# The low part of each gate product on GpSimd, half passes in groups of six, and three smaller moves

## The chip, the cores and the metric

One core of a Trainium2 chip. The metric is the device time of one execution in microseconds, the median of several runs. The engines are named as in the profile: PE is TensorE (matrix products; PEld its weight loads), DVE is VectorE, ACT is ScalarE, POOL is GpSimd, SP is SyncE, which here only issues DMAs.

## What is computed

Cut to what matters, `x` is 2048 tokens of 448 features:

```python
xn = layernorm(x)
a  = irfft2(rfft2(xn) * (w_r + 1j * w_i), s=(2048, 448))   # 2048 x 225 spectral weights
h  = relu(xn @ W_gate) * (xn @ W_up)                        # 448 x 1792 each
return x + a + h @ W_down                                   # 1792 x 448
```

All of it is done in float32 accuracy from float16 products: each operand is split into a high and a low float16 part, and three products (high·high, high·low, low·high) are summed in PSUM.

## The kernel before, in words

Two jobs share the engines. The foreground is the gated feed-forward part. The 1792 hidden features are 14 blocks of 128, in groups of 5, 5 and 4; the tokens are four chunks `q` of 512, in the order 0, 2, 1, 3. A *unit* `(f, q)` is one block for one chunk: ten products for the gate and ten for the up half (`gu_full`, L712), each 128 rows by 512 columns. For every group and chunk the units of the group are followed, a little later, by four *down* products (`dn_mm`, L775), 448 columns wide, which read the high and low part of all the group's units.

448 features are three and a half tiles of 128 rows, in a high and a low part. The odd half tiles are products with 64 rows, the *half passes* (`gu_half`, L718): one gate and one up half pass for each unit, on different rows of TensorE, so that two can run at once. They stand in groups: the first unit of a pair does its full products, then come the half passes of its mate (which opens the mate's PSUM banks) and its own, then the mate's full products (`gu_halves`, L740). `mates` (L969) holds the pairs.

After a unit, `gu_post` (L766) makes its result: ScalarE takes the rectified gate out of PSUM (`gu_relu`, L752), VectorE multiplies by the up half (`gu_times`, L756), ScalarE writes the float16 high part `h` (`gu_hi`, L760), and VectorE the low part, the difference (`gu_lo`, L764). The first five units belong to an opening that is written out by hand (`OPENING`).

PSUM has eight banks: two buffers of two banks for units (`gu`), two for down products (`dn`), two for the background (`fx`).

The background is the layer norm of the later chunks and the Fourier part. It is a list of small steps (`bg`); `run_bg` puts so many of them behind each unit that VectorE's time, by a table of costs, is a fixed share of TensorE's (`fixed`, `room`, L1096 to L1110). Its butterflies (`bfly`, L391) work on 18 buffers with a list of free ones. `swap` (L539) and `row_in` (L556) copy rows between partitions by DMAs.

GpSimd has little to do: small copies in the layer norm (`ln_copy`, `ln_copy_lo`), some fills, and one sum over all partitions (`all_sum`, L188) for each block of gate and up weights, for each group of down weights and for the spectral weights. These all-reduces give the scales: ScalarE squares the weights (L186), GpSimd sums, VectorE turns the sum into a power of two (L192, L196) with which the weights are then split.

Each engine works through its own instructions in the order in which a scheduler put them when the program was built; between engines there are semaphores.

Of the kernel before, what the change touches and what calls it, by code (L numbers as in the profile page):

```python
# [133 lines left out]
def tile_gfnet_reglu(ctx: ExitStack, tc: tile.TileContext, x, xr, wgu, wd, wf, wrow, ident, c_fd, c_fm, c_im, c_row, c_id,  # L134
# [10 lines left out]
    def fx():  # L145
        return psum.tile([128, 512], F32, name="fx", bufs=2)
# [184 lines left out]
    def ln_tp(n2, tiles):  # L331
        if n2 not in tp:
            tp[n2] = fx().bitcast(F16).rearrange("p (a b) -> p a b", b=128)
        for a in tiles:
            P.transpose(tp[n2][:, a, :], tt[n2][:, a, :], id_t)
# [9 lines left out]

    zps, eo, X, Xh, yps, cur = {}, {}, {}, {}, {}, {}

    def f_dft(n2):
        q, j = n2 % 4, n2 // 4
        js = slice(128 * j, 128 * (j + 1))  # L350
        ps = fx()
# [33 lines left out]
    def f_sdft(n2):  # L385
        y = yps[n2] = fx()[:, 0:XW].rearrange("p (g c k) -> p g c k", g=4, c=2)
        m, xh = fm_t[n2 % 8][:, n2 // 8], Xh[n2 % 8][:, n2 // 8]
        for i, (a, b) in enumerate(((0, 0), (0, 1), (1, 0))):
            P.matmul(y, m[:, a, :], xh[:, b], start=(i == 0), stop=(i == 2), skip_group_check=True)  # L389

    def bfly(a, b, p, sgn):  # L391

        if p == 0:
            t = free.pop()
            V.tensor_tensor(t, a, b, op=OP.add)  # L395
            V.tensor_tensor(b, a, b, op=OP.subtract)  # L396
            free.append(a)
            return t, b
        t = free.pop()
        if p == 4:  # L400
# [5 lines left out]
            free.append(b)  # L406
# [132 lines left out]
    def swap(key, k):  # L539
# [27 lines left out]
    def row_dft(d):  # L567
        y = state["rowps"] = fx()
# [35 lines left out]
    def i_sdft(n2):  # L604
        ps = fx()
# [20 lines left out]
    def i_ddft(n2):  # L626
        ps = fx()
# [81 lines left out]
    def gu_open(f, q):  # L709
        hps[f, q] = psum.tile([128, 2, 512], F32, name="gu", bufs=2)  # L710

    def gu_full(f, q, gs, cs, start, stop, seq=SEQ):  # L712
        for g in gs:
            for i, (a, b) in enumerate(seq):
                last["P"] = P.matmul(hps[f, q][:, g, cs], wt[f, g][:, a, :], Tq[q][:, b, cs],  # L715
                                     start=(start and i == 0), stop=(stop and i == len(seq) - 1)).ins

    def gu_half(f, q, g, start, prev):  # L718
# [3 lines left out]
        m = P.matmul(hps[f, q][:, g, 0:512], wt[f, g][rows, 7, :], Tq[q][rows, b, :], start=start, stop=not start).ins  # L722
# [7 lines left out]
    def gu_unit(f, q, mate):  # L730
# [7 lines left out]
        gu_halves(f, q, mate)  # L738
# [11 lines left out]
    def gu_relu(f, q):  # L750
        g1s[f, q] = mt([128, 512], F32, "g1", 3)
        last["A"] = A.activation(g1s[f, q], hps[f, q][:, 0, :], AF.Relu, scale=2.0 ** -22).ins  # L752

    def gu_times(f, q):
        g1 = g1s[f, q]
        last["V"] = V.scalar_tensor_tensor(g1, hps[f, q][:, 1, :], 2.0 ** -22, g1, op0=OP.mult, op1=OP.mult).ins  # L756
# [5 lines left out]
    def gu_lo(f, q):  # L762
        h = ht[f, q]
        V.tensor_tensor(h[:, 1, :], g1s.pop((f, q)), h[:, 0, :], op=OP.subtract)  # L764
# [10 lines left out]
    def dn_mm(fs, n2, c0=0, c1=D):  # L775
        q, j = n2 % 4, n2 // 4
        js = slice(128 * j, 128 * (j + 1))
        ps = psum.tile([128, 512], F32, name="dn", bufs=2)
# [180 lines left out]
    gseq = [("gu", g, f, q) for g, fs in enumerate(groups) for q in CHUNKS for f in fs]  # L959
    units, pend = [], []  # L960
    for k, u in enumerate(gseq):
        units.append(u)
        if k % 2 and pend:
# [5 lines left out]
    mates = {u: v for u, v in zip(gseq[::2], gseq[1::2])}  # L969
# [80 lines left out]
    def gu_slab(f, g):  # L1050
        if f % 2 == 0 and g == 0:
            gu_open(f, q)
        gu_full(f, q, (g,), slice(0, 512), f % 2 == 0, f % 2 == 1)

    for f in groups[0]:
# [9 lines left out]
        if f % 2 == 0:  # L1065
            piece(f"hp{f}", gu_halves, f, q, mates["gu", 0, f, q][2:])
# [13 lines left out]
    with tc.manual_schedule(engines={mybir.EngineType.PE, mybir.EngineType.DVE, mybir.EngineType.Activation,  # L1080
# [3 lines left out]
        wps = psum.tile([128, 512], F32, name="dn", bufs=2)  # L1084
# [11 lines left out]
    def fixed(i):  # L1096
        c = 1.37 if units[i][0] == "gu" else 0.68
# [21 lines left out]
    for i, u in list(enumerate(units))[len(groups[0]):]:  # L1119
        is_gu = u[0] == "gu"  # L1120
        parts = [(0, D)] if i < len(units) - 1 else [(0, CUT), (CUT, D)]
        if is_gu:
            _, g, f, q = u
            run_bg(until=marks["T", q])
            gu_unit(f, q, (mates.get(u) or (0, 0, None, None))[2:])
# [74 lines left out]
```

## Time and profile before

| | us |
|---|---|
| median of 3 runs (446.71 to 446.97) | 446.72 |
| the profiled execution's own time | 446.92 |
| its span | 445.1 |
| TensorE busy | 438.4 (98%) |
| VectorE busy | 373.5 (84%) |
| ScalarE busy | 178.9 (40%) |
| GpSimd busy | 32.9 (7%) |

The span runs from the first to the last instruction of the profiled execution; 1.8 us of its time lie around it. In the lines of groups the columns are: source line, engine, operation, what it writes from what, shape and count; then busy microseconds and mean nanoseconds of one; then the idle time ahead of them and who ended it. In the lines of the timeline and of the chain they are start and length in microseconds. Where several instructions that follow each other make one line, the length goes from the first one's start to the last one's end. TensorE's products overlap each other, so their rate is read from starts and not from lengths.

### The profile page before, as it was taken

How to read it: one execution, taken by the hardware profiler on the slowest of the kernel's cores; microseconds unless marked ns; L12 is line 12 of the kernel's file. 1: busy time of each engine (PE TensorE's matmuls, PEld its weight loads, DVE VectorE, ACT ScalarE, POOL GpSimd, SP SyncE). 2: the span in 40 equal slices, each digit the busy share in tenths (PEclk: the TensorE clock that was granted, in tenths of full speed). 3: DMA queues.
4: the chain of work that ended last, by engine and by line, in shares of the span. 5: the costliest groups of instructions: out<-in, count | busy, mean ns of one | idle time of the engine just before them, and what ended most of it. 6: DMA issues, size and time to landing. Idle time of an engine off the chain costs nothing.

```text
span 445.1 us, 7091 instructions
## 1 busy us (share of the span) xinstructions
PE 438.4 (98%) x2630; PEld 218.8 (49%) x2630; DVE 373.5 (84%) x802; ACT 178.9 (40%) x365; POOL 32.9 (7%) x97
## 2 busy tenths in 40 slices
PE   8999999999999999999999999999999999999997
PEld 3543554444546444444444444444444455556565
DVE  5988696998858979999999999896997997766364
ACT  5886252351543666043233145344142242233230
POOL 2431031040000120000000010000000000000000
DMA  8929966041001261432220021000001333231113
GB/s 271 323 52 282 371 217 119 1 90 41 0 14 61 95 222 34 133 105 62 85 80 6 1 84 55 0 13 0 14 0 42 93 96 90 55 96 34 63 43 124
DMA packets 37115, 39.72 MB, mean 89 GB/s; under 512 B 17927, under 2 KB 32473, under 8 KB 37081
## 3 DMA queue, kind: packets, MB, share of 16 engines
q1 hardware_dynamic: 35928, 37.40, 27.4%
q10 hardware_dynamic: 1152, 1.87, 2.1%
q8 instruction: 20, 0.33, 0.3%
q14 instruction: 15, 0.11, 0.1%
HBM read 24.45 MB, written 3.67 MB: 63 GB/s over the span
## 4 chain that ended last, share of the span: by engine, by line
PE 91%; DVE 3%; DMA 2%; ACT 1%; issue 1%; POOL 1%; SPq 0%; ACTq 0%
PE gu L715 50%; PE dn L783 29%; PE gu L722 3%; PE fx L611 2%; PE fx L357 2%; PE fx L632 2%; PE fx L389 2%; DMA y<-in_xr 1%; DMA T<-tt 1%; DVE bst L248 1%; DVE wt L669 1%; DVE y L291 0%; DVE g L756 0%; ACT T L341 0%; DVE tt L320 0%
## 5 line engine op out<-in xcount | busy, mean ns | idle before, releaser
L715 PE MATMUL gu<-T,wt 128*128 128x512 f16 (+1 forms) x1140 | 256.1, 375 | 0.0
L715 PEld LDWEIGHTS <-wt 128*128 128x128 f16 x1140 | 108.7, 98 | 129.8 <-issue 9.3
L783 PE MATMUL dn<-wdt,h 128*128 128x448 f16 (+2 forms) x684 | 136.4, 349 | 0.0
L783 PEld LDWEIGHTS <-h 128*128 128x128 f16 x684 | 65.8, 98 | 59.9
L752 ACT ACTIVATE g<-gu 128x512 f32<-128x512 f32 x56 | 33.2, 594 | 115.1 <-PE gu L722 77.4
L760 ACT ACTIVATE h<-g 128x512 f16<-128x512 f32 x56 | 35.0, 627 | 47.3 <-DVE g L756 47.3
L756 DVE SCALAR_TENSOR_TENSOR g<-gu,g 128x512 f32<-128x512 f32 x56 | 38.5, 687 | 11.4 <-ACT g L752 11.3
L790 DVE SCALAR_TENSOR_TENSOR xy<-dn,dsc,xy 128x448 f32<-128x448 f32 (+2 forms) x49 | 32.9, 671 | 15.1 <-PE dn L783 14.8
L764 DVE TENSOR_TENSOR h<-g,h 128x512 f16<-128x512 f32 x56 | 38.5, 689 | 4.9 <-ACT h L760 4.8
L665 ACT ACTIVATE wt<-wst,wsc 128x512 f16<-128x512 f32 x28 | 19.1, 716 | 15.7 <-DVE wsc L196 15.7
L669 DVE SCALAR_TENSOR_TENSOR wt<-wst,wsc,wt 128x512 f16<-128x512 f32 x28 | 20.5, 749 | 0.0
L637 DVE SCALAR_TENSOR_TENSOR xy<-fx,fsc,xy 128x448 f32<-128x448 f32 x16 | 10.8, 681 | 10.7 <-PE fx L632 10.7
L189 POOL PARTITION_ALL_REDUCE wm<-wm x15 | 7.8, 521 | 158.9 <-ACT junk L186 158.9
L396 DVE TENSOR_TENSOR y<-y 128x456 f32<-128x456 f32 x22 | 13.9, 631 | 4.8 <-DMA row<-y 4.5
L722 PE MATMUL gu<-T,wt 64*128 64x512 f16 x112 | 17.0, 381 | 0.8 <-DMA T<-tt 0.7
L186 ACT ACTIVATE junk<-wst 128x512 bf16<-128x512 f32 x28 | 17.4, 622 | 0.2
L595 ACT ACTIVATE vt<-y,fsc 128x912 f16<-128x912 f32 x8 | 8.4, 1052 | 20.7 <-PE fx L611 12.3
L618 ACT ACTIVATE wf<-fx 114x512 f16<-114x512 f32 x16 | 9.4, 588 | 17.4 <-PE fx L611 16.6
L553 DVE TENSOR_TENSOR y<-y,sw 128x456 f32<-128x456 f32 x16 | 10.1, 628 | 5.7 <-DMA sw<-y 5.7
L395 DVE TENSOR_TENSOR y<-y 128x456 f32<-128x456 f32 x22 | 13.8, 628 | 0.2
L611 PEld LDWEIGHTS <-vt 128*128 128x128 f16 x192 | 12.0, 98 | 3.3
L611 PE MATMUL fx<-wf,vt 128*128 128x128 f16 x192 | 13.2, 219 | 0.0
(115 smaller groups left out, 431.4 us busy)
## 6 DMA issues: line engine op xcount, KB each, us to landing
wst<-in_wgu SPq DMA_DIRECT2D x28, 256.0 KB
wf<-in_wf SPq DMA_DIRECT2D x8, 456.0 KB
sw<-y SPq DMA_DIRECT2D x16, 224.4 KB
y<-in_xr SPq DMA_DIRECT2D x16, 224.0 KB
xy<-in_x SPq DMA_DIRECT2D x16, 224.0 KB
out<-xy SPq DMA_DIRECT2D x15, 224.0 KB
wdst<-in_wd SPq DMA_DIRECT2D x14, 224.0 KB
sw<-y SPq DMA_DIRECT2D x8, 228.0 KB
```

What stands on the lines that cost most here:

```text
L186: A.activation(o, src, AF.Square, scale=SQ, accum_out=acc)
L611: P.matmul(o, v[:, h, w], m[:, c, :], start=(i == 0), stop=(i == 2), skip_group_check=True)
L665: A.activation(w[:, 0:4, :], wst[f, g], AF.Copy, scale=wsc[f, g])
L669: V.scalar_tensor_tensor(w[:, 4:8, :], st, sc, w[:, 0:4, :], op0=OP.mult, op1=OP.subtract)
L715: last["P"] = P.matmul(hps[f, q][:, g, cs], wt[f, g][:, a, :], Tq[q][:, b, cs], start=(start and i == 0), stop=(stop and i == len(seq) - 1 ...
L722: m = P.matmul(hps[f, q][:, g, 0:512], wt[f, g][rows, 7, :], Tq[q][rows, b, :], start=start, stop=not start).ins
L752: last["A"] = A.activation(g1s[f, q], hps[f, q][:, 0, :], AF.Relu, scale=2.0 ** -22).ins
L756: last["V"] = V.scalar_tensor_tensor(g1, hps[f, q][:, 1, :], 2.0 ** -22, g1, op0=OP.mult, op1=OP.mult).ins
L760: A.activation(ht[f, q][:, 0, :], g1s[f, q], AF.Copy)
L764: V.tensor_tensor(h[:, 1, :], g1s.pop((f, q)), h[:, 0, :], op=OP.subtract)
L783: last["P"] = P.matmul(ps[:, 0:c1 - c0], ht[f, q][:, a, js], wdt[f][:, b, c0:c1], start=(i == 0), stop=(i == n - 1)).ins
L790: last["V"] = V.scalar_tensor_tensor(o, dps[n2][:, 0:c1 - c0], dsc[:, g:g + 1], o, op0=OP.mult, op1=OP.add).ins
```

## The change

Five edits:

1. The low part (`gu_lo`) of every unit after the opening is a GpSimd instruction instead of a VectorE one.
2. The half passes stand in groups of three units (six half passes) instead of two, but for the first two and the last two groups. Units and down products share a ring of six single banks, since three units are open at once. Full products are held behind the group's last half pass.
3. In butterflies without a twiddle factor the difference goes over the first operand instead of the second, and freed buffers go to the other end of the list.
4. One of two copies of the forward swap and the copies of `row_in` are issued from ScalarE's queue instead of SP's.
5. The planner charges a unit 0.69 us of VectorE's time instead of 1.37, and asks for 6 us more room.

```diff
-        return psum.tile([128, 512], F32, name="fx", bufs=2)
+    RINGS = {'gu': ('gu', 6), 'dn': ('gu', 6), 'fx': ('fx', 2)}
+    def bank(name="fx"):
+        tag, n = RINGS[name]
+        return psum.tile([128, 512], F32, name=name, tag=tag, bufs=n)
...
     def bfly(a, b, p, sgn):
         if p == 0:
             t = free.pop()
             V.tensor_tensor(t, a, b, op=OP.add)
-            V.tensor_tensor(b, a, b, op=OP.subtract)
-            free.append(a)
-            return t, b
+            V.tensor_tensor(a, a, b, op=OP.subtract)
+            free.insert(0, b)
+            return t, a
...
         if key == "X":
             nc.sync.dma_start(t[1:64], u[65:128])
-            nc.sync.dma_start(t[64:128], u[0:64])
+            nc.scalar.dma_start(t[64:128], u[0:64])
...
-            nc.sync.dma_start(row[p:p + 8, 0, :], cur["s1", j, par][64:65].rearrange("p g c k -> p (g c) k"))
+            nc.scalar.dma_start(row[p:p + 8, 0, :], cur["s1", j, par][64:65].rearrange("p g c k -> p (g c) k"))
...
     def gu_open(f, q):
-        hps[f, q] = psum.tile([128, 2, 512], F32, name="gu", bufs=2)
+        hps[f, q] = [bank("gu") for g in range(2)]
...
-    def gu_halves(f, q, mate):
-        gu_open(*mate)
+    def gu_halves(f, q, mates):
         m = last["P"]
-        for i in range(4):
+        vs = [v[2:] for v in mates] + [(f, q)]
+        for i in range(2 * len(vs)):
+            v = vs[i // 2]
+            if i % 2 == 0 and v != (f, q):
+                gu_open(*v)
+                opened.add(v)
             with tc.high_priority(offset=2000 if i else 0):
-                m = gu_half(*((f, q) if i > 1 else mate), 1 - i % 2, i < 2, m)
-        opened.add(mate)
+                m = gu_half(*v, 1 - i % 2, v != (f, q), m)
+        last["half"] = m
...
     def gu_lo(f, q):
         h = ht[f, q]
-        V.tensor_tensor(h[:, 1, :], g1s.pop((f, q)), h[:, 0, :], op=OP.subtract)
+        e = G if "opened" in state and q in CHUNKS else V
+        e.tensor_tensor(h[:, 1, :], g1s.pop((f, q)), h[:, 0, :], op=OP.subtract)
...
+    for n in [2, 2] + [3] * 16 + [2, 2]:
+        mates[gseq[k]] = gseq[k + 1:k + n]
...
     def fixed(i):
-        c = 1.37 if units[i][0] == "gu" else 0.68
+        c = 0.69 if units[i][0] == "gu" else 0.68
...
-        lo, hi = (m, hi) if sum(room(i, m) for i in range(RAMP, last_gu)) < need else (lo, m)
+        lo, hi = (m, hi) if sum(room(i, m) for i in range(RAMP, last_gu)) < need + 6.0 else (lo, m)
```

The new kernel's line numbers are up to 14 higher: L764 becomes L773, L722 becomes L726, L189 becomes L192.

Two places show what the scheduler made of it. The first is TensorE at a group of half passes for chunk 2, with the numbers of the tiles. Before, two units' half passes stand together, the gate and up half of each in one two-bank tile:

```order
L722 LDWEIGHTS wt_423
L722 MATMUL gu_868<-T2_63,wt_423 128x512
L722 LDWEIGHTS wt_401
L722 MATMUL gu_868<-T2_63,wt_401 128x512
L722 LDWEIGHTS wt_326
L722 MATMUL gu_847<-T2_63,wt_326 128x512
L722 LDWEIGHTS wt_314
L722 MATMUL gu_847<-T2_63,wt_314 128x512
```

Now those of three units, each half with a bank of its own:

```order
L726 MATMUL gu_928<-T2_63,wt_422 128x512
L726 LDWEIGHTS wt_456
L726 MATMUL gu_927<-T2_63,wt_456 128x512
L726 LDWEIGHTS wt_546
L726 MATMUL gu_932<-T2_63,wt_546 128x512
L726 LDWEIGHTS wt_520
L726 MATMUL gu_931<-T2_63,wt_520 128x512
L726 LDWEIGHTS wt_425
L726 MATMUL gu_906<-T2_63,wt_425 128x512
L726 LDWEIGHTS wt_403
L726 MATMUL gu_905<-T2_63,wt_403 128x512
```

So there are 20 groups in place of 28, with the same 112 half passes.

The second is GpSimd where the all-reduces for the last four blocks' weights stand. Rows with `ISA` and a `wm` tile are the all-reduces. Before, they follow each other, between that for the down weights of the second group (`wdm_2099`) and that of the third (`wdm_3289`):

```order
L189 ISA wdm_2099<-wdm_2099 128x5
L189 ISA wm_2852<-wm_2852 128x2
L189 ISA wm_2902<-wm_2902 128x2
L189 ISA wm_2945<-wm_2945 128x2
L189 ISA wm_3088<-wm_3088 128x2
L189 ISA wdm_3289<-wdm_3289 128x4
```

Now the low parts (L773, into an `h` tile) stand among them. The rows `ISA` without a tile name one of two libraries of GpSimd code, which the program puts ahead of an instruction whose code is in the other one: the all-reduce's is library 1, the subtraction's library 0.

```order
L773 TENSOR_TENSOR h_2837<-g1_2834,h_2837 128x512
L192 ISA
L192 ISA wm_2950<-wm_2950 128x2
L773 ISA
L773 TENSOR_TENSOR h_2875<-g1_2872,h_2875 128x512
L192 ISA
L192 ISA wm_2993<-wm_2993 128x2
L773 ISA
L773 TENSOR_TENSOR h_2915<-g1_2912,h_2915 128x512
L773 TENSOR_TENSOR h_2967<-g1_2964,h_2967 128x512
```

Between any all-reduce and a low part there is now such a row: 26 in all, against one before, which stands ahead of the first all-reduce in the opening.

More of the change, by code (lines that the diff above doesn't have):

```diff
@@ L626, in i_ddft @@
     def i_ddft(n2):
-        ps = fx()
+        ps = bank()
         h = pgh[n2]
@@ L714, in gu_full @@
             for i, (a, b) in enumerate(seq):
-                last["P"] = P.matmul(hps[f, q][:, g, cs], wt[f, g][:, a, :], Tq[q][:, b, cs],
+                m = last["P"] = P.matmul(hps[f, q][g][:, cs], wt[f, g][:, a, :], Tq[q][:, b, cs],
                                      start=(start and i == 0), stop=(stop and i == len(seq) - 1)).ins
+                if "opened" in state and "half" in last:
+                    tc.add_manual_dep(m, last["half"].name, NOSYNC, reason="half passes stand together")
     def gu_half(f, q, g, start, prev):
         rows, b = TOP[g]
-        m = P.matmul(hps[f, q][:, g, 0:512], wt[f, g][rows, 7, :], Tq[q][rows, b, :], start=start, stop=not start).ins
+        m = P.matmul(hps[f, q][g], wt[f, g][rows, 7, :], Tq[q][rows, b, :], start=start, stop=not start).ins
         if "opened" in state:
@@ L777, in dn_mm @@
         js = slice(128 * j, 128 * (j + 1))
-        ps = psum.tile([128, 512], F32, name="dn", bufs=2)
+        ps = bank("dn")
         n = 3 * len(fs)
@@ L1083, in tile_gfnet_reglu @@
         G.memset(warm, 0.0)
-        wps = psum.tile([128, 512], F32, name="dn", bufs=2)
+        wps = bank("dn")
         gu_open(0, q)
```

40 lines of the change are left out of this document (21 added, 19 removed).

## The prediction

> **What bounds the kernel now.** I read the page's busy times first, then TensorE by stage, then TensorE's own groups.
>
> ```profile
> PE 438.4 (98%) x2630; PEld 218.8 (49%) x2630; DVE 373.5 (84%) x802; ACT 178.9 (40%) x365; POOL 32.9 (7%) x97
> 50.00:150.00 100.00, 100.00 (x632) 51.04 (x629) 85.37 (x209) 42.66 (x88) 13.64 (x37) 1.00 0.31 88
> 150.00:250.00 100.00, 100.00 (x498) 45.61 (x496) 95.43 (x196) 39.20 (x89) 3.52 (x7) 1.00 0.28 86
> 250.00:350.00 100.00, 100.00 (x499) 45.82 (x497) 87.88 (x183) 34.54 (x72) 2.96 (x5) 1.00 0.10 28
> 350.00:445.00 95.00, 92.25 (x753) 53.94 (x751) 65.84 (x109) 27.87 (x43) 0.00 (x0) 1.00 0.25 76
> ```
>
> In the stages (columns: length, then busy time of TensorE, its weight loads, VectorE, ScalarE and GpSimd, granted clock, DMA) TensorE is busy all the time at full clock, but for the last 2.75 us, when its work is done. From 50 us on nothing holds it up, so a faster neighbour gains nothing there. Only fewer or cheaper TensorE instructions can shorten the run, and only a late operand can lengthen it. GpSimd looks almost free: 7%. What this share hides is the question of this case.
>
> **Half passes: what the change takes away.** TensorE around one group of today, four half passes:
>
> ```profile
> 155.67 0.81 PE L715 MATMUL gu<-T,wt 128*128 128x512 f16 x3
> 156.31 0.35 PE L783 MATMUL dn<-wdt,h 128*128 128x448 f16 x1
> 156.60 0.61 PE L722 MATMUL gu<-T,wt 64*128 64x512 f16 x4
> 157.14 0.75 PE L389 MATMUL fx<-Xh,fm 128*128 128x456 f16 x3
> 157.72 4.48 PE L715 MATMUL gu<-T,wt 128*128 128x512 f16 x20
> 162.04 1.11 PE L783 MATMUL dn<-wdt,h 128*128 128x448 f16 x5
> 162.99 0.38 PE L715 MATMUL gu<-T,wt 128*128 128x512 f16 x1
> ...
> L722 PE MATMUL gu<-T,wt 64*128 64x512 f16 x112 | 17.0, 381 | 0.8 <-DMA T<-tt 0.7 <-DVE wt L669 0.2
> ```
>
> Starts give the true rates: a gate/up product (162.04 − 157.72)/20 = 0.216 us, a down product (162.99 − 162.04)/5 = 0.19 us. The down product ahead of the group takes 0.29 (156.31 to 156.60), so entering costs 0.10. The group lasts 0.54 to the next start. The last half starts 0.61 − 0.38 = 0.23 after the first: two halves run at once, and a pair more costs 0.23. A group of four is 0.10 + 0.54 = 0.64 us, a group of six 0.87. Today there are 28 groups, 17.9 us; after the change 4 of four and 16 of six, 2.6 + 13.9 = 16.5 us. The gain is **1.4 us**, all on the path, since TensorE is the path. Its unknown is small: a third pair could cost the 0.10 of a transition again, which would leave nothing of it.
>
> **Six banks, butterflies, ScalarE's copies, the planner.** A bank of the shared ring is written again, by the new order, 4.5 us of TensorE time after it was last filled, at the closest (21 gate/up products); emptying it takes the rectifier and the product below, 0.59 + 0.69 us. The cover is three times the need: nothing.
>
> ```profile
> L752 ACT ACTIVATE g<-gu 128x512 f32<-128x512 f32 x56 | 33.2, 594 | 115.1 <-PE gu L722 77.4 <-PE gu L715 37.5 <-DVE h L764 0.2
> L756 DVE SCALAR_TENSOR_TENSOR g<-gu,g 128x512 f32<-128x512 f32 x56 | 38.5, 687 | 11.4 <-ACT g L752 11.3
> L760 ACT ACTIVATE h<-g 128x512 f16<-128x512 f32 x56 | 35.0, 627 | 47.3 <-DVE g L756 47.3
> L764 DVE TENSOR_TENSOR h<-g,h 128x512 f16<-128x512 f32 x56 | 38.5, 689 | 4.9 <-ACT h L760 4.8
> 341.62 0.67 ACTq L548 DMA_DIRECT2D sw<-y  x1
> ```
>
> The butterflies keep count and size and change only which buffer is freed. 24 DMA issues move from SP to ScalarE, 0.67 us each by the last row, 16 us on an engine that is 40% busy; queued behind them are rectifiers, whose banks have some 3 us to spare: nothing, or 0.67 each where the spare is gone. The planner's smaller charge per unit moves background work on VectorE and is paid by the low parts that leave it: 51 × 0.689 = 35 us.
>
> **The low part on GpSimd.** Its own length has no row. GpSimd's nearest is filling a tile of 512, 0.52 us; two operands in and one out, each at that rate, would be 1.6. I take 1.1.
>
> ```profile
> L1083 POOL MEMSET warm<- 128x512 f16 x1 | 0.5, 524 | 0.0
> 63.56 1.41 POOL L304 COPY tt<-tt 128x48 f16<-128x48 f16 x1 [0.63 <-ACT tt L300]
> 65.09 0.22 POOL L309 COPY tt<-tt 128x48 f16<-128x48 f16 x1
> ...
> 63.60 0.55 DVE L320 TENSOR_TENSOR tt<-y,tt 128x384 f16<-128x384 f32 x1
> 64.07 0.22 DVE L321 TENSOR_TENSOR tt<-y,tt 128x64 f16<-128x64 f32 x1
> 64.20 0.55 DVE L320 TENSOR_TENSOR tt<-y,tt 128x384 f16<-128x384 f32 x1
> 64.67 0.22 DVE L321 TENSOR_TENSOR tt<-y,tt 128x64 f16<-128x64 f32 x1
> ...
> L395 DVE TENSOR_TENSOR y<-y 128x456 f32<-128x456 f32 x22 | 13.8, 628 | 0.2
> L413 DVE SCALAR_TENSOR_TENSOR y<-y 128x228 f32<-128x228 f32 x16 | 6.3, 392 | 0.0
> L419 DVE SCALAR_TENSOR_TENSOR y<-y 128x456 f32<-128x456 f32 x20 | 12.6, 630 | 0.3
> ```
>
> A copy of 48 columns takes 0.22 us, and 1.41 when VectorE runs four instructions with two operands in SBUF over it: the two engines wait for each other. In the new order the low part of a unit is read at the earliest 6 us after the unit's end, in the last group, and 6.8 us before it. Ahead of it lie the product, 0.7, and then such a run on VectorE, the longest after a product 2 × 0.628 + 4 × 0.392 + 2 × 0.630 = 4.1 us, which covers the high part, and 1.1: some 6. So the distance covers it, barely; in the last group VectorE has no such runs. If each low part held VectorE for its whole 1.1, the stage from 150 on, with about 13 of them, would go from 95.4 to 95.4 − 9 + 14.3 = 101 of 100 us: about 1 us late. [...]
>
> **The code swaps: what the change adds.** In front of the first all-reduce stands an instruction without operands that names a code library. Before, there is one in the whole run. Afterwards all-reduces (one library) and low parts (another) alternate in GpSimd's row, and each change of kind has its swap: 25 in the main part besides the one in the opening. GpSimd works in order, so a swap holds up all behind it. Its only row:
>
> ```profile
> 7.38 0.24 POOL L305 COPY tt<-tt 128x64 f16<-128x64 f16 x1
> 7.86 0.39 POOL L189 PARTITION_ALL_REDUCE wm<-wm  x1 [0.25 <-ACT junk L186]
> ...
> L189 POOLq MODIFY_POOL_CONFIG  x2: 11/11/11, 7.6 to 7.7; - x2
> ...
> L1082 ACT ACT_TABLE_LOAD x1 | 1.3, 1283 | 0.7 <-PEq L1188 0.7
> ...
> 3.09 4.49 DMA y<-in_xr
> ```
>
> Between the copy's end at 7.62 and the all-reduce at 7.86 lie both configuration records and 0.25 us. That bounds a swap from below. But in a run that uses only this library, it can be in place from the execution before: the row may show a swap with nothing to fetch. The nearest rows of fetching are ScalarE's table load, 1.28 us, and the landing of the x tiles, 4.49. An upper end is two such transfers, 9.0, one for each of the two records. I take a fetch and a load, 4.49 + 1.28 = **5.8 us**, an estimate. [...]
>
> Where it decides is the last place shown of GpSimd's order. The squares that an all-reduce waits for, on ScalarE:
>
> ```profile
> L186 ACT ACTIVATE junk<-wst 128x512 bf16<-128x512 f32 x28 | 17.4, 622 | 0.2
> L186 ACT ACTIVATION_READ_ACCUMULATOR junk<-wst 128x1 f32 x28 | 5.3, 190 | 0.0
> ```
>
> Count from the end of unit A (low part h_2837). With 0.216 per gate/up product, 0.87 per group of six and 0.19 per down product, the units B, C, D (h_2875, h_2915, h_2967) end at 4.4, 8.7 and 13.9 us, and the down products that read the low parts of B, C, D start at 20.2, 20.7 and 21.3. GpSimd: the first all-reduce is ready when ScalarE has squared the next weights after A's rectifier, about 2.2 (0.59 + 2 × (0.62 + 0.19)), and ends at 2.6; then swap 8.4, A 9.5, swap 15.3, all-reduce 15.7, swap 21.5, B 22.6 (2.4 late), swap 28.4, all-reduce 28.8, swap 34.6, C 35.7 (20.7 + 2.4 was needed: 12.6 late), D 36.8 (0.5 late). Five swaps S lie between 2.6 and C: the stall is 5S − 14, **15.5 us** at 5.8, nothing below 2.8.
>
> Near 110 us stands the other dense run, with h_1395, h_1521 and h_1644 at its end. Its first swap now follows the copies of the last x tiles, which today are done at 97.9:
>
> ```profile
> 97.64 0.24 POOL L305 COPY tt<-tt 128x64 f16<-128x64 f16 x1
> 110.65 0.44 POOL L189 PARTITION_ALL_REDUCE wm<-wm  x1 [11.89 <-ACT junk L186]
> ...
> 108.56 4.42 PE gu L715 x20
> ```
>
> From there to low part h_1521 lie six swaps, three all-reduces, two copies and three low parts: 6S + 5 us, so 137.7 at 5.8. It is read, by the same count of products, 19.4 us after the end of unit h_1395, which ends at 112.98 by the last row: 132.4. Late by **5 us**; nothing below S = 4.9. The other swaps of the main part lie where units are 10 us and more apart; only that ahead of the filter's all-reduce, for which VectorE waits, shows: 0 to 5.8, I take 2.
>
> The opening: an execution now ends with the other library in place, so the first all-reduce finds its swap real.
>
> ```profile
> 9.78 0.14 DVE L192 TENSOR_SCALAR eg<-wm 128x1 uint32<-128x1 uint32 x1
> 1.54 5.68 PE L1023 MATMUL dn<-warm 128*128 128x512 f16 x13 [1.54 <-POOL warm L1083]
> ```
>
> The all-reduce would end at 7.7 + 5.8 + 0.4 = 13.9 instead of 8.25; VectorE reads it at 9.78, and its queue waits **4.1 us**, with the copies of x behind the swap as late. And a TensorE that stood idle may run slow: at the start 13 products take 5.68/13 = 0.44 us each instead of 0.216, 2.9 us lost. Five stalls make 0 to 14; I take 5.
>
> Sum: 446.92 (this execution: span 445.1 and 1.8 around it) − 1.4 + 4.1 + 5 + 15.5 + 2 + 5 = 477.1; the median before, 446.72, is 0.2 lower, so **476.9**.
>
> **Rivals.** *The swap costs what its one row shows* (0.25 or less). Then nothing above 2.8 is reached, the low parts come in time, and only the half passes remain: 446.7 − 1.4 = **445.3**, faster. For it: the one measured swap. Against it: that one may have had nothing to do. 0.27.
>
> *A swap between 2.2 and 2.9 us, or cheap swaps with VectorE and GpSimd in each other's way*: the opening's S − 1.7, or the 1 us of the stage from 150, eats the gain: **446.7**, no change. Two rows of 1.28 would make 2.6. 0.07.
>
> *Slower by the swaps*: 0.66. Its own range: at S = 3.5, 3.5 from the run near 260, 1.8 in the opening, −1.4 and some clock: 452; at S = 7.3, 22.5 near 260, 14 near 110, 5.6 in the opening, 4 at the filter and 7 of clock, −1.4: about 499. At 9.0 it would be past 520.
>
> **Numbers.** Predicted 476.9. About 0.2% is what a measurement of this kernel tells from no change. The range must take in the faster rival, since leaving it out leaves out more than 2 in 10: 444.8 to 500; the likeliest case's own is 452 to 500. Faster 0.27, same 0.07, slower 0.66.
>
> **What would show it.** Right: GpSimd's row with some 5 us idle before the first low part after an all-reduce; TensorE's down products around 270 waiting for GpSimd; TensorE below 100% in 110 to 140 and 250 to 350, with a granted clock under 1; the first product of the opening 4 us later. Wrong: gaps of 0.3 us around the configuration records and TensorE still at 100%, with groups of six half passes at 0.87 us; then the run is at 445. If low parts come late without a swap ahead of them, it is the shared access to SBUF.

## The result, and the profile after

The changed kernel takes **503.19 us** (median of 6 runs, 502.40 to 504.31) against 446.85 (446.46 to 447.00): 1.126 times as long, 95% interval 1.1249 to 1.1279. The forecast was 476.9, its range 444.8 to 500.0: the direction and the main mechanism were right, the time lies 3.2 us beyond the range.

The profiled execution, span 501.2 us. First the busy times, then TensorE by stage (columns as in the prediction: start and end, length, busy time of TensorE, its weight loads, VectorE, ScalarE and GpSimd, granted clock, DMA), then five short stretches by themselves.

```profile
PE 448.9 (90%) x2630; PEld 222.6 (44%) x2630; DVE 365.2 (73%) x751; ACT 177.2 (35%) x365; POOL 98.7 (20%) x148
50.00:150.00 100.00, 89.65 (x544) 45.18 (x543) 70.19 (x163) 35.09 (x74) 22.89 (x45) 0.94 0.38 105
150.00:250.00 100.00, 95.25 (x500) 44.84 (x499) 89.88 (x179) 38.55 (x87) 21.64 (x20) 0.97 0.30 89
250.00:350.00 100.00, 80.77 (x382) 35.82 (x381) 72.62 (x131) 31.58 (x71) 16.61 (x15) 0.88 0.10 27
350.00:450.00 100.00, 95.99 (x602) 48.99 (x600) 74.73 (x144) 27.56 (x44) 18.75 (x15) 0.98 0.20 53
...
16.90:21.90 5.00, 4.97 (x19) 2.46 (x20) 4.59 (x19) 3.97 (x8) 2.33 (x8) 0.50 0.03 11
146.00:151.60 5.60, 5.60 (x16) 2.11 (x17) 0.68 (x1) 0.00 (x0) 1.02 (x1) 0.50 0.00 0
226.80:230.10 3.30, 3.28 (x9) 0.97 (x9) 3.27 (x6) 1.23 (x2) 1.54 (x1) 0.50 0.09 35
320.20:325.70 5.50, 5.50 (x15) 2.05 (x16) 2.99 (x7) 0.00 (x0) 1.03 (x1) 0.50 0.00 0
383.70:387.20 3.50, 3.49 (x10) 1.02 (x10) 3.50 (x9) 0.62 (x1) 2.73 (x1) 0.51 0.00 0
```

TensorE, busy all the time before, is now at 81 to 96% of the stages, and it is the two stages with dense all-reduces that lose most. GpSimd, the reason, is only 20% busy: the share of busy time still hides the case. The five stretches are those just behind a stall; there TensorE works at half the clock. They are 22.9 us long and so cost about another 11.4 (half of their length).

Who waits (time in all, number, longest), and TensorE's row around its two worst places:

```profile
PEld L792 <- POOL h L773: 32.5, 5, 14.4
PE dn L792 <- POOL h L773: 29.6, 3, 13.6
POOL h L773 <- issue: 50.1, 7, 7.6
...
134.51 1.11 PE L792 MATMUL dn<-wdt,h 128*128 128x448 f16 x5
145.96 6.16 PE L792 MATMUL dn<-wdt,h 128*128 128x448 f16 x17 [10.35 <-POOL h L773]
...
305.25 1.30 PE L792 MATMUL dn<-wdt,h 128*128 128x448 f16 x3 [5.61 <-POOL h L773]
320.18 6.10 PE L792 MATMUL dn<-wdt,h 128*128 128x448 f16 x17 [13.62 <-POOL h L773]
```

Down products wait 29.6 us for GpSimd's low parts. GpSimd's own row ahead of these two places; the number in brackets is the idle time before the instruction, and "issue" means that nothing which the profile shows was waited for:

```profile
115.99 1.15 POOL L773 TENSOR_TENSOR h<-g,h 128x512 f16<-128x512 f32 x1 [6.71 <-ACT junk L189]
123.11 0.41 POOL L192 PARTITION_ALL_REDUCE wm<-wm  x1 [5.96 <-ACT zc L366]
130.22 1.15 POOL L773 TENSOR_TENSOR h<-g,h 128x512 f16<-128x512 f32 x1 [6.70 <-ACT zc L366]
137.31 0.41 POOL L192 PARTITION_ALL_REDUCE wm<-wm  x1 [5.95 <-issue]
144.76 2.26 POOL L773 TENSOR_TENSOR h<-g,h 128x512 f16<-128x512 f32 x2 [7.04 <-issue]
...
288.98 1.15 POOL L773 TENSOR_TENSOR h<-g,h 128x512 f16<-128x512 f32 x1 [6.73 <-ACT junk L189]
296.04 0.44 POOL L192 PARTITION_ALL_REDUCE wm<-wm  x1 [5.92 <-ACT h L768]
304.06 1.14 POOL L773 TENSOR_TENSOR h<-g,h 128x512 f16<-128x512 f32 x1 [7.57 <-issue]
311.02 0.41 POOL L192 PARTITION_ALL_REDUCE wm<-wm  x1 [5.83 <-ACT wf L498]
318.98 2.26 POOL L773 TENSOR_TENSOR h<-g,h 128x512 f16<-128x512 f32 x2 [7.55 <-issue]
```

Between any two instructions of different kinds in the main part lies a change of code: 5.8 to 6.0 us to the all-reduce, 6.7 to 7.6 us back to the subtraction, where what follows was ready. A pair of changes cost 13 us here; the work between them is an all-reduce of 0.4 and a low part or two of 1.15. Whatever the brackets name as releaser, the gaps are the same.

### The profile page after: what moved, and what is told of

The parts are those of the page before. It is cut to its first block, busy times and chain, and to the rows that moved or that the text cites. A ratio compares the mean times of both kernels' runs of the same rounds, so it can differ in the third digit from the quotient of the medians.

```text
span 501.2 us, 7222 instructions
## 1 busy us (share of the span) xinstructions
PE 448.9 (90%) x2630; PEld 222.6 (44%) x2630; DVE 365.2 (73%) x751; ACT 177.2 (35%) x365; POOL 98.7 (20%) x148
## 4 chain that ended last, share of the span: by engine, by line
PE 65%; DVE 15%; issue 9%; DMA 5%; ACT 4%; POOL 1%; POOLq 0%; DVEq 0%; ACTq 0%
PE gu L717 34%; PE dn L792 21%; DMA sw<-y 3%; PE gu L726 2%; PE fx L359 2%; PE fx L613 2%; PE fx L391 2%; ACT junk L189 2%; DVE g L764 2%; PE fx L634 1%; DVE xy L799 1%; DVE wdt L703 1%; DMA row<-y 1%; POOL h L773 1%; PE dn L1036 1%
## 5 line engine op out<-in xcount | busy, mean ns | idle before, releaser
L792 PE MATMUL dn<-wdt,h 128*128 128x448 f16 (+2 forms) x684 | 138.8, 360 | 29.6 <-POOL h L773 29.6
L773 POOL TENSOR_TENSOR h<-g,h 128x512 f16<-128x512 f32 x51 | 67.8, 1332 | 276.3 <-ACT h L768 199.1
L792 PEld LDWEIGHTS <-h 128*128 128x128 f16 x684 | 67.0, 100 | 94.1 <-POOL h L773 32.5
L764 DVE SCALAR_TENSOR_TENSOR g<-gu,g 128x512 f32<-128x512 f32 x56 | 38.3, 685 | 30.2 <-ACT g L760 24.0
L726 PE MATMUL gu<-T,wt 64*128 64x512 f16 x112 | 17.5, 392 | 9.3 <-DVE g L764 8.4
L671 DVE SCALAR_TENSOR_TENSOR wt<-wst,wsc,wt 128x512 f16<-128x512 f32 x28 | 22.0, 809 | 1.1 <-ACT wt L667 1.1
L192 POOL PARTITION_ALL_REDUCE wm<-wm x15 | 6.6, 442 | 76.4 <-issue 26.3
L189 ACT ACTIVATE junk<-wst 128x512 bf16<-128x512 f32 x28 | 17.4, 621 | 3.0 <-DMA wst<-in_wgu 2.8
L397 DVE TENSOR_TENSOR y<-y 128x456 f32<-128x456 f32 x22 | 16.1, 733 | 1.6 <-DMA row<-y 1.5
L421 DVE SCALAR_TENSOR_TENSOR y<-y 128x456 f32<-128x456 f32 x20 | 15.1, 758 | 0.2
L398 DVE TENSOR_TENSOR y<-y 128x456 f32<-128x456 f32 x22 | 15.0, 680 | 0.2
L624 DVE SCALAR_TENSOR_TENSOR wf<-fx,wf 114x512 f16<-114x512 f32 x16 | 10.8, 683 | 4.5 <-ACT wf L620 4.5
```

What stands on the lines that cost most here:

```text
L189: A.activation(o, src, AF.Square, scale=SQ, accum_out=acc)
L671: V.scalar_tensor_tensor(w[:, 4:8, :], st, sc, w[:, 0:4, :], op0=OP.mult, op1=OP.subtract)
L726: m = P.matmul(hps[f, q][g], wt[f, g][rows, 7, :], Tq[q][rows, b, :], start=start, stop=not start).ins
L764: last["V"] = V.scalar_tensor_tensor(g1, hps[f, q][1], 2.0 ** -22, g1, op0=OP.mult, op1=OP.mult).ins
L773: e.tensor_tensor(h[:, 1, :], g1s.pop((f, q)), h[:, 0, :], op=OP.subtract)
L792: last["P"] = P.matmul(ps[:, 0:c1 - c0], ht[f, q][:, a, js], wdt[f][:, b, c0:c1], start=(i == 0), stop=(i == n - 1)).ins
```

## Experiments

Theory A is the prediction's: the change of GpSimd's code is the cost, paid by what waits behind it. Its rivals came with the runs: the other edits, the loading itself, access to SBUF, the planner. Times are medians; the kernel before took 446.9 to 447.1 beside them. Unless said otherwise a kernel is the changed one with the edit shown.

**e1 and e2: the change without GpSimd's low parts.**

```diff
-        e = G if "opened" in state and q in CHUNKS else V
+        e = V
-        c = 0.69 if units[i][0] == "gu" else 0.68
+        c = 1.37 if units[i][0] == "gu" else 0.68
-        lo, hi = (m, hi) if sum(room(i, m) for i in range(RAMP, last_gu)) < need + 6.0 else (lo, m)
+        lo, hi = (m, hi) if sum(room(i, m) for i in range(RAMP, last_gu)) < need else (lo, m)
 e2 besides:
-    for n in [2, 2] + [3] * 16 + [2, 2]:
+    for n in [2] * 28:
```

Expected of e1: 

> The low part is back on VectorE and the planner's charge back at 1.37 without the 6 us; groups of three, six banks, butterflies and ScalarE's DMA issues stay. Theory 1 (swaps of GpSimd's code library make the whole loss): no swap is left but the opening's, which has nothing to fetch; TensorE at 100% from 50 us on, and the gain of the half passes is there: 446.85 - 1.4 = 445.4 us. Theory 2 (low parts and VectorE's instructions hold each other up at SBUF): the same 445.4. Theory 3 (the ring of six banks makes TensorE wait): TensorE still waits ahead of groups of half passes, 9 us or more in all, 455 or more.

Expected of e2: 

> As e1_vector, but the half passes in groups of two units again, still on the ring of six banks. Theory 1: a group of four costs 0.64 us and 28 of them 17.9, so 1.4 us more than e1_vector: 446.8, no change against before. If a third pair pays its transition again, e1_vector has no gain over this one.

Measured: e1 451.47 us (ratio 1.0097, 1.0082 to 1.0112), e2 451.22 (1.0093, 1.0078 to 1.0108). Both missed on the slow side, e1 by 6.1 us and e2 by 4.4. So 52 of the 56 us go with the low parts and the planner's numbers for them, but the edits taken for harmless are not harmless, and groups of three gain nothing over pairs. See e5 to e7, e12, e14 to e16.

**e3 and e4: low parts on GpSimd with few changes of code.** In e3 the main part's all-reduces are a GpSimd copy, which leaves out the sum over the partitions; in e4 only the last twelve units' low parts go to GpSimd (planner as in e1).

```diff
 e3:
-        G.partition_all_reduce(o, i, 128, bass_isa.ReduceOp.add)
+        if "opened" in state:
+            G.tensor_copy(o, i)
+        else:
+            G.partition_all_reduce(o, i, 128, bass_isa.ReduceOp.add)
 e4:
-        e = G if "opened" in state and q in CHUNKS else V
+        e = G if f in groups[2] and q != CHUNKS[0] else V
```

Expected of e3: 

> The changed kernel with every all-reduce after the opening replaced by a copy on GpSimd; the sum over partitions is left out there, so scales differ by partition and the output is not the reference's. Low parts stay on GpSimd. One swap is left in the main part, ahead of the first low part, and the one in the opening, which is real since the execution before ended with the other library. Theory 1: 445.4, plus the opening's 7.4 us wait and up to 3 us of slow clock behind it: 453 to 456. Theory 2: the low parts still take 1.15 us and more and lengthen VectorE's instructions, so most of the loss stays: 485 or more. Theory 3: 460 or more.

Expected of e4: 

> Low parts on GpSimd only for the last twelve units, behind the last all-reduce; planner's charge as before the change. One swap in the main part with nothing behind it for long, and an execution ends with the other library in place. Theory 1: the opening's swap is real, all else is free: 453 to 456. If the opening's swap were free whatever ran before: 445.4. Theory 2: twelve of 51 low parts, a quarter of the loss: about 459.

Measured: e3 459.54 (1.0277, 1.0256 to 1.0298), e4 458.61 (1.0262, 1.0245 to 1.0279). The opening's change is the only change of code that TensorE is seen to wait for, and both stand 7 to 8 us above e1. Both lie above theory 1's 453 to 456, since its base, 445.4, was wrong by e1's 6 us; e3 is far below the 485 of theory 2 (shared access to SBUF), but e4 alone would also fit that theory's 459. e8, next, tells them apart. The main part's changes, with the waits for its all-reduces, are worth 503.2 − 459.5 = 43.7 us.

**e8: the opening.** The kernel of e4, with the all-reduce's code put back at the end:

```diff
+        if f == NF - 1 and q == CHUNKS[-1]:
+            all_sum(g1[:, 1:2], g1[:, 0:1])
```

> The kernel of e4 (low parts on GpSimd in the last twelve units alone) with one all-reduce more after the last low part, into a column that nothing reads, so that the program ends with the all-reduce's code loaded as the program of before does. If the 7 to 8 us between e1 and e4 are one change of code at the start, paid because the execution before left the other code behind: the wait ahead of the first all-reduce falls from 8.0 to 0.25 us, the opening's stall goes, and the time is 458.6 - 7.4 = 451.2 us (450.5 to 452). If the start pays whatever was left behind, or the 7 us lie in the last units: 458.6 us still, or 459 to 460 with the added change of code at the end.

Measured: 450.98 (1.0093, 1.0079 to 1.0107), 7.6 us less than e4 and within the range for a change at the start: twelve low parts cost nothing that is seen here, which rules out theory 2's share. The opening of the changed kernel, then that of e8, and e8's end:

```profile
16.13 0.40 POOL L192 PARTITION_ALL_REDUCE wm<-wm  x1 [8.60 <-issue]
16.93 0.29 PE L338 MATMUL fx<-id_t,tt 128*128 128x128 f16 x1 [7.17 <-POOL tt L308]
```

```profile
7.73 0.38 POOL L192 PARTITION_ALL_REDUCE wm<-wm  x1 [0.24 <-ACT junk L189]
...
437.65 0.40 POOL L192 PARTITION_ALL_REDUCE g<-g  x1 [5.84 <-issue]
```

The code that one execution ends with is in place for the next: the idle time ahead of the first all-reduce is 8.60 us in the changed kernel and 8.00 in e4, which end with the subtraction, and 0.24 in e8, which ends with an all-reduce. So the one row of before, 0.25 us, was a change to code already in place, as the prediction suspected; the change at e8's end, 5.84 us under the last products, holds nothing up.

**e9 and e10: the first rival's world.** e9 is e3 with e8's lines; no path holds a change of code. e10 has the planner's old numbers besides.

```diff
 e10 besides:
-        c = 0.69 if units[i][0] == "gu" else 0.68
+        c = 1.37 if units[i][0] == "gu" else 0.68
-        lo, hi = (m, hi) if sum(room(i, m) for i in range(RAMP, last_gu)) < need + 6.0 else (lo, m)
+        lo, hi = (m, hi) if sum(room(i, m) for i in range(RAMP, last_gu)) < need else (lo, m)
```

Expected of e9: 

> The kernel of e3 (low parts on GpSimd, main all-reduces replaced by a GpSimd copy, so that no code changes in the main part) with one real all-reduce more at the very end, so that the next execution starts with the all-reduce's code loaded, as e8 did: GpSimd carries every low part and no change of code is on any path. It is the world of the prediction's first rival, which put 445.3 us on it. Theory A (by e3, e4, e8): the opening's 7.5 us go from e3's 459.5 us: 452.0 us (451 to 453), so the offload brings nothing even for free, since TensorE is busy without a break. Rival's 445.3 us: 444.8 to 446.5.

Expected of e10: 

> The kernel of e9 with the planner's two numbers of before (1.37 us of VectorE time for each unit, no 6.0 us added). If those two numbers overfill VectorE's row and so cause e3's waits of 1.5 and 3.1 us in the half passes (VectorE's gate product late, its bank held): 449 to 450.5 us. If they don't matter (the prediction's 0): as e9, within 1 us.

Measured: e9 452.65 (1.0126, 1.0113 to 1.0139), e10 454.88 (1.0177, 1.0152 to 1.0203). Even with no change of code on its path the kernel is slower than before: the rival's 445.3 would not have come true in its own world. The planner's new numbers help here, by 2.2 us between the medians, so both answers expected of e10 missed; TensorE's waits for VectorE's gate product stay, 4.5 us in e9 and 4.3 in e10. With the planner's numbers alike (e10 against e1), the low parts on GpSimd cost 3.4 us even where no code changes on the path.

**e11: changes of code with nothing behind them.** The kernel of e1, and in front of every all-reduce of the main part, placed right behind the one before, a small GpSimd addition (and late in the program one VectorE instruction that reads its result):

```diff
+            m = G.tensor_tensor(zero[:, 0:4], zero[:, 0:4], zero[:, 4:8], op=OP.add)
+            tc.add_manual_dep(m.ins, last["G"].name, NOSYNC, reason="code changed twice")
```

> The kernel of e1 (low parts on VectorE) with a GpSimd addition of 128x4 zeros behind each all-reduce of the main part, so that the code changes twice between any two all-reduces, 24 changes in all, as in the changed kernel, but no low part stands behind one. Theory A (a change of code costs nothing by itself, only what waits behind it pays): 451.5 us, 453 at most. Rival (the loading slows the chip, its memory or its clock, whoever waits): a large part of the 44 us between e3 and the changed kernel, 470 us or more. Between: all-reduces late by a pair of changes, and VectorE waiting for them: 455 to 465.

Measured: 462.97 (1.0345, 1.0315 to 1.0376), 11.5 above e1. Where they come from, by the waits of TensorE and VectorE and by a long stretch with changes of code, in e11 (first fence) and the same work in e1 (second):

```profile
PE gu L732 <- DMA T<-tt: 4.2, 2, 3.4
PE gu L732 <- DVE g L770: 2.9, 2, 2.0
...
DVE eg L201 <- POOL wm L198: 8.9, 2, 8.4
...
120.00:300.00 180.00, 179.05 (x939) 84.53 (x938) 156.95 (x328) 72.48 (x162) 9.48 (x20) 1.00 0.22 64
```

```profile
115.00:295.00 180.00, 178.65 (x940) 84.44 (x938) 163.46 (x342) 74.24 (x166) 8.27 (x13) 1.00 0.22 64
```

Through those 180 us the code changes 15 times and TensorE does the same work (939 and 940 instructions, busy for 179.05 and 178.65 us) at a mean clock of 1.00 in both: here the changes by themselves slowed neither TensorE's work nor its clock. The rest comes from two places where somebody did wait after all (copies of x late for TensorE near 113 us, a scale for which VectorE waited 8.4 us up to 303 and, behind it, TensorE for VectorE's gate products between 309 and 315) and from a slow clock, seen behind the second: five gate/up products begun at 316.22 take 2.31 us, against 1.24 at a granted clock of 1.00 (e16, from 225.73); the mean granted clock of the whole run is 0.991. What theory A says of a change by itself holds; its 453 was too low, since all-reduces and copies stand in that queue too, and the time fell in the range put on those waits, 455 to 465.

**e13: low parts behind the changes, and nobody waiting for an all-reduce.** The kernel of e9, with

```diff
         if "opened" in state:
             G.tensor_copy(o, i)
+            G.partition_all_reduce(spare[:, 0:i.shape[-1]], i, 128, bass_isa.ReduceOp.add)
```

> The kernel of e9 (every low part on GpSimd, scales from a copy in place of the main all-reduces, one all-reduce at the very end) with a real all-reduce behind each copy, into a tile that nothing reads: GpSimd's row changes code as in the changed kernel and low parts stand behind the changes, but nobody waits for an all-reduce. Theory A (late low parts are the larger part of the main part's 43 us, and waits for all-reduces some 11): 452.7 + 32 = 485 us (478 to 492), with TensorE's down products waiting for GpSimd. Rival (the waits for the all-reduces, through VectorE's row, are the larger part): 465 us or less.

Measured: 496.69 (1.111, 1.1085 to 1.1134), 44.0 above e9, more than expected. TensorE's waits:

```profile
PE dn L801 <- POOL h L780: 37.3, 6, 13.1
PE gu L732 <- DVE g L770: 4.0, 3, 2.5
```

Late low parts alone make as much as the whole main part lost (43.7). The waits for all-reduces, 11.5 us in e11, hardly add to that: e13 and the opening's 7.6 us give 496.7 + 7.6 = 504.3 against the changed kernel's 503.2. But the two kernels don't lose it in the same places: TensorE waits 37.3 us for low parts here and 29.6 in the changed kernel, where it also waits 8.4 for VectorE's gate products (4.0 here). How the changed kernel's 43.7 us divide between late low parts and late all-reduces is not shown.

**e5, e6, e7, e12, e14, e15, e16: the 4.5 us of e1.** All with low parts on VectorE and the planner's old numbers. e5, e6, e14 and e15 start from e2: e5 divides the ring again; e14 undoes ScalarE's DMA issues, e15 the butterflies, e6 both; e16 is e6 with groups of three; e7 and e12 add a rule to e16.

```diff
 e5:
-    RINGS = {'gu': ('gu', 6), 'dn': ('gu', 6), 'fx': ('fx', 2)}
+    RINGS = {'gu': ('gu', 4), 'dn': ('dn', 2), 'fx': ('fx', 2)}
 e6, e14 (DMA issues):
-            nc.scalar.dma_start(t[64:128], u[0:64])
+            nc.sync.dma_start(t[64:128], u[0:64])
...
 e6, e15 (butterflies):
-            V.tensor_tensor(a, a, b, op=OP.subtract)
-            free.insert(0, b)
-            return t, a
+            V.tensor_tensor(b, a, b, op=OP.subtract)
+            free.append(a)
+            return t, b
...
 e7 (e12: three, in the last group alone):
+                if i == 0 and len(posts) >= 2:
+                    tc.add_manual_dep(last["P"], posts[-2].name, NOSYNC, reason="two products in flight")
```

Expected of e5: 

> The kernel of e2 (low parts on VectorE, half passes in pairs) with its PSUM banks divided again: four for gate and up, two for the down products, as before; butterflies and ScalarE's DMA issues stay as changed. Theory A (the shared ring of six costs the 4.5 us of e1 and e2: down products no longer wait for a bank, are laid into TensorE's row ahead of the filter's inverse, and the inverse's last 24 products come out behind them at the end): 446.5 to 447.5 us, and TensorE's row ends with down products as it did before the change. Theory B (ScalarE's DMA issues or the butterflies cost it): 451 us still.

Expected of e6: 

> The kernel of e2 with the butterflies and the DMA issues as before the change, and the shared ring of six kept: the ring is the only edit left in it. Theory A: 451 us (450.5 to 451.5), TensorE's row ending with 24 products of the inverse. Theory B: 446.5 to 447.5 us.

Expected of e7: 

> Low parts on VectorE, half passes in groups of three on the ring of six, butterflies and DMA issues as before the change, and one rule more: a down product's first matmul is laid behind the second last down product's eviction, so that at most two are under way, as two banks made it before. Theory A: the 4.5 us go and the groups of three bring their 1.4 us: 445.4 us, 447.0 at most. If the order alone doesn't cost it (theory B, here: the ring's banks are held by something else), 450 to 451.5 us.

Expected of e12: 

> The kernel of e7 with its rule in the last group of hidden slices alone, and three down products under way rather than two: half passes in groups of three, ring of six, butterflies and DMA issues as before the change. In the row that results, a half row of down products stands behind the inverse's last 24. Theory A (1.9 us of the ring's cost is the end, where the inverse's sums and stores follow the last matmul; the rest are waits): 3.1 us behind the last matmul instead of 5.0, and 446.5 to 448.5 us. If the end isn't where it is lost: 449.5 to 451.

Expected of e14: 

> The kernel of e2 (pairs, ring of six, low parts on VectorE) with the 24 DMA issues back on SP, the butterflies as changed. If ScalarE's issues cost the 1.7 us between e2 and e6: 449.5 us. If the butterflies do: 451.2 us.

Expected of e15: 

> The kernel of e2 with the butterflies as before the change and ScalarE's DMA issues kept. If ScalarE's issues cost the 1.7 us: 451.2 us. If the butterflies do: 449.5 us. If each costs a part: both of these runs near 450.3 us.

Expected of e16: 

> The kernel of e6 (ring of six, nothing else of the change) with half passes in groups of three instead of pairs. If the groups bring the prediction's 1.4 us: 448.1 us. If the third unit's bank is held by a gate product that VectorE makes late, so that a group waits inside: 449 to 450 us, with gaps of about 1 us inside one or two groups of half passes.

| kernel | us (lowest to highest) | ratio to before (95%) |
|---|---|---|
| e5 two rings | 449.38 (449.19 to 450.23) | 1.0056 (1.0043 to 1.0069) |
| e6 ring alone | 449.51 (449.16 to 450.00) | 1.0056 (1.0043 to 1.0069) |
| e14 DMA issues back | 449.28 (448.88 to 450.06) | 1.0052 (1.0039 to 1.0065) |
| e15 butterflies back | 449.60 (449.18 to 450.04) | 1.0059 (1.0047 to 1.0071) |
| e16 threes alone | 451.76 (450.08 to 451.81) | 1.0094 (1.0081 to 1.0108) |
| e7 two in flight | 450.34 (450.16 to 451.15) | 1.0076 (1.0064 to 1.0089) |
| e12 three in flight | 449.60 (449.31 to 450.45) | 1.0058 (1.0046 to 1.0070) |

The end of TensorE's row, before the change and in e6 (the spans end at 445.1 and 448.2):

```profile
438.54 1.35 PE L632 MATMUL fx<-idc_t,wf 114*128 114x112 f16 x24
439.73 2.52 PE L783 MATMUL dn<-wdt,h 128*128 128x288 f16 x24
```

```profile
441.10 0.66 PE L792 MATMUL dn<-wdt,h 128*128 128x288 f16 x4
442.04 1.35 PE L634 MATMUL fx<-idc_t,wf 114*128 114x112 f16 x24 [0.28 <-DVE xy L639]
...
442.83 1.28 DVE L639 SCALAR_TENSOR_TENSOR xy<-fx,fsc,xy 128x448 f32<-128x448 f32 x2 [0.24 <-PE fx L634]
444.03 1.39 DVE L799 SCALAR_TENSOR_TENSOR xy<-dn,dsc,xy 128x448 f32<-128x448 f32 x3
```

With six banks down products no longer wait for one of two, are laid into the row earlier, and the filter's inverse comes last. The last five evictions (VectorE's instructions that take sums out of PSUM), begun beside its last products, and their stores then end the run. The last matmul starts 3.1 us before the end of the span before, 5.0 us in e6: 1.9 us, most of the 2.5 by which e6 is slower. This is read from the traces; no run changes the end alone, and e5 and e6 came out between what their two theories said. In e5 the row ends as before (3.1 us again), but with four banks for gate and up the groups of half passes fall apart, 34 instead of 28; its 449.4 says nothing against the end. e7 and e12 restore part of the order (3.1 and 4.2 us), came out where their expectations put a cost that does not lie in the order or the end, and have waits among the inverse's products (in e12 also one of 1.0 us in a group of half passes): they don't confirm the end as the cause, nor rule it out. Undoing either the DMA issues or the butterflies takes off as much as undoing both, 1.6 to 1.9 us: no one edit owns it, and why the pair costs it stays open. In e16 a group of three waits, and another falls apart:

```profile
186.83 0.60 PE L726 MATMUL gu<-T,wt 64*128 64x512 f16 x3
187.87 0.59 PE L726 MATMUL gu<-T,wt 64*128 64x512 f16 x3 [0.44 <-DVE g L764]
...
226.91 0.60 PE L726 MATMUL gu<-T,wt 64*128 64x512 f16 x3
227.44 0.23 PE L573 MATMUL fx<-rowh,row_t 128*128 128x57 f16 x2
227.60 0.60 PE L726 MATMUL gu<-T,wt 64*128 64x512 f16 x3
```

Two of the sixteen groups come out in halves with other products between, two wait for a bank that VectorE's gate product holds. That takes up most of the 1.4 us of gain in this execution (450.66 us); that e16's median lies 2.2 us above e6, and above the 449 to 450 expected with such waits, is not explained by it and stays open. None of the kernels beats the one before.

## Why the prediction was right or wrong

The path was right and the sum was not. The step that failed is the reckoning of the edits outside GpSimd, −1.4 us for the half passes and nothing for the six banks ("The cover is three times the need: nothing"), the butterflies and ScalarE's DMA issues: together they measured 4.5 us slower (e1). Two more terms were mis-sized: the slow clock, about 11.4 us in place of 5, and the change of code back to the subtraction, 6.7 to 7.6 us in place of 5.8. Term by term:

- **The mechanism** (low parts late behind changes of code, the opening's change real since the execution before leaves the other code behind): right, by e3, e8, e11 and e13.
- **S = 5.8 us**: right in one direction, 5.83 to 6.00 in the changed kernel; 6.7 to 7.6 back, which the prediction had no row for. That a transfer of x and ScalarE's table load add up to the first figure is luck as far as is known: no run shows what a change is made of. *Near 260* the five changes took 33.6 us in place of 29.0, so the 15.5 us become 20.1; measured 5.61 + 13.62 = 19.2. *Near 110* six took 38.3 in place of 34.8, so 5 become 8.5; measured 10.35. *Opening*: 8.60 in place of 5.8, so 4.1 become 6.9; measured 7.17. The count of what stands in GpSimd's row was right; the term was mis-sized.
- **The filter's all-reduce, 2 us**: VectorE waited 5.8 us for it, and the group of half passes begun at 379.4 then 3.7 for VectorE's product; e13, without that wait, has no such stall there, which points to it without showing it.
- **Slow clock, 5 us**: about 11.4, or 2.3 for each of five stretches. The prediction had the price of one (2.9 from the opening's products) and the number, five, and then took 5 out of "0 to 14" without a row that says so.
- **Half passes, −1.4**: the group's price was right, 0.10 + 0.75 = 0.85 us for six by e7's starts (0.87 forecast). The sum was wrong: e16 is not faster than e6. What failed is the cover of "three times the need": emptying a bank takes 0.59 + 0.69 = 1.3 us once started, but VectorE's row starts it late, behind background work.
- **Six banks, butterflies, ScalarE's DMA issues: 0**: with the groups of three 4.5 us (e1); the ring alone 2.5 (e6). The prediction asked what a bank costs, not what order more banks give. Why the butterflies and the DMA issues cost the rest only together stays open.
- **The planner, 0**: it gains 2.2 us with the low parts on GpSimd (e9 against e10).
- **The low part, 1.1 us**: 1.14 at least, 1.33 on average. That VectorE and GpSimd hold each other up was put at about 1 us; e9 stands 1.2 above e1, but with the planner's 2.2 in its favour: low parts without changes of code cost 3.4 (e10 against e1).

From 476.9, the terms' differences: opening 3.1, near 110 5.4, near 260 3.7, filter 1.7, clock 6.4, edits outside GpSimd 5.9 (4.5 in place of −1.4), low parts and planner together 1.2: 27.4, so 504.3. One slow stretch (226.8 to 230.1, about 1.65 us) has its like in e9 and so is counted twice; without it 502.6, against 503.2. The clock and the edits outside GpSimd are the largest. The range's upper end still held the −1.4, and the 5.9 us alone are more than the 3.2 by which it was missed.

## What to carry to other kernels

Before work goes to an idle engine, read that engine's row, not its share: GpSimd, at 7% before, paid 13 us here for each pair of changes between two kinds of code, and it was the queue behind the change that paid. A relief for an engine off the critical path was worth nothing by itself here (e9), while an order that a scheduler makes can turn with a freed resource (e6): look at the end of the program. A stall can also cost what the clock takes back after it, about 11.4 us here in five stretches at a granted clock of 0.50 to 0.51.

## What the runs showed of the hardware

**VectorE and GpSimd held each other up in SBUF.** VectorE and GpSimd of the changed kernel in the same 6 us:

```profile
263.97 0.69 DVE L764 SCALAR_TENSOR_TENSOR g<-gu,g 128x512 f32<-128x512 f32 x1
265.60 0.63 DVE L420 SCALAR_TENSOR_TENSOR y<-y 128x456 f32<-128x456 f32 x1
266.27 1.60 DVE L421 SCALAR_TENSOR_TENSOR y<-y 128x456 f32<-128x456 f32 x1
...
263.53 1.48 POOL L773 TENSOR_TENSOR h<-g,h 128x512 f16<-128x512 f32 x1 [3.60 <-ACT h L768]
266.23 1.16 POOL L773 TENSOR_TENSOR h<-g,h 128x512 f16<-128x512 f32 x1 [1.22 <-ACT h L768]
```

L421, with both operands in SBUF, takes 1.60 us beside a low part and 0.63 alone; L764, one of whose operands is in PSUM, takes 0.69 beside one, as always (0.67 to 0.69 in all 56). The low part itself takes 1.14 us at the shortest, 1.16 in the median, and 3.79 at the longest (begun at 384.47, under a run of VectorE's instructions with both operands in SBUF). Taking for each of VectorE's instructions the time above the median of its line, those that lie beside a low part lost 22.3 us, nearly all in 28 instructions. The low parts relieve VectorE of 51 × 0.69 = 35 us, so about two thirds come back. By what the two hold each other up is not shown.

**The clock.** In the changed kernel a wait of TensorE of 1.71 us (up to 209.6) left the clock as it was (1.00 from 207.2 to 212.7); behind the waits of 3.04, 3.68, 7.17, 10.35 and 13.62 us it worked for 3.3 to 5.6 us at half clock (the five stretches above, granted 0.50 to 0.51), a gate/up product at 0.43 us instead of 0.22. The three products behind the wait of 5.61 us, up to the next wait, were granted 0.50 as well. But the length of the wait alone does not decide it: e3 and e9 have the same wait of 3.04 us in the same group of half passes, and only e9 was slow behind it (0.96 us for three half passes against 0.59). First e3, then e9, three half passes each:

```profile
210.97 0.59 PE L729 MATMUL gu<-T,wt 64*128 64x512 f16 x3 [3.04 <-DVE g L767]
```

```profile
205.06 0.96 PE L729 MATMUL gu<-T,wt 64*128 64x512 f16 x3 [3.04 <-DVE g L767]
```

Nor does the clock column show every slow stretch: the first 13 products of the kernel before start 0.43 us apart, up to 7.06 us, under a granted clock of 1.00.

**Code.** Copies and fills ran on GpSimd under either code without a change. In the changed kernel copies stand right behind an all-reduce (that of 16.13, copies at 16.41 and 16.58, the next all-reduce at 16.79) and right behind a low part (that of 99.96, copies from 101.07 on), 0.22 to 0.55 us each, with no idle time shown between; the fills from 180.54 on stand between two low parts, and in the kernel before between two all-reduces. The 26 changes all stand ahead of an all-reduce or a low part (in e11 an all-reduce or an addition).
